# Layer 1 of a fused attention and MLP kernel: one set of four tiles by half products in blocks 3 to 6, fixed staging tiles, and another place for the check of the bounds

## The chip, the cores and the metric

The kernel runs on one core of a Trainium2 chip. Its time is the device time of one execution in microseconds; several runs are given by their median. The engines are called TensorE (PE in the profile, its weight loads PEld), VectorE (DVE), ScalarE (ACT), GpSimd (POOL) and SyncE (SP).

## The reference

Eight batches of 576 tokens. Attention of 8 heads of 64 columns each, causal, with 16 beacon keys and values in front that every token sees; then a low-rank mix over the tokens, and a two-layer MLP with a residual:

```python
scores = scale * q @ concat(beacon_k, k).T        # causal on k; beacons always seen
a = softmax(scores);  x = a @ concat(beacon_v, v) # x: (8, 576, 512) after joining the heads
u = x + ((x.T @ U) @ V).T                         # U (576, 32), V (32, 576)
out = u + relu(u @ w_ch1) @ w_ch2                 # w_ch1 (512, 2048), w_ch2 (2048, 512), float32 out
```

The kernel computes in 16-bit floats with sums in float32.

## The kernel before, in words

**Two interleaved streams.** The attention goes by pairs of heads (`p` = 4 x batch + pair), the MLP by nine blocks of 512 tokens out of the 4608. The MLP's work is cut into units, closures in a list `queue`; `fill(n)` takes n of them and issues their instructions. The order of issue is written out by hand: `long_slot` (L1383) gives for each pair of heads from batch 3 on where the scores (`go`), the masks, the weighting of the two heads (`weighted`), the mix and the `fill`s stand. One batch takes 30 units, and a block has 30. The pattern of one batch puts units 3 to 12 of a block beside pair 3, units 13 to 15 and the first two of layer 2 beside pair 0, the next nine beside pair 1, and the rest and units 0 to 2 of the next block beside pair 2. Every engine works through its own instructions in the order of issue.

**Layer 1.** `g_unit(k)` (L628): 16 units for 16 tiles of 128 of the 2048 hidden columns; each is four matmuls of 512 tokens into one PSUM bank (L635), then a rectifying eviction to the tile `gT` on ScalarE (L646) or, in units 2, 5, 11 and 13, on VectorE (L644). `u` lies transposed in a ring `uT` of 4 x 576 columns (L163); where a block crosses the ring's end, in block 4 at its middle, each matmul is two of 256 columns (`u_cols`, L165).

**Layer 2.** A product of 512 x 2048 by 2048 x 512, done as seven products of halves instead of eight (`products`, L827). `sums` (L617) builds on VectorE the sums of halves of `gT` that this takes (L624); `SUMS` (L1164) says after which unit, with 16 and up for layer 2. `c_unit(k, j)` (L833) is half j of product k, 14 units, called c0 to c13 here; `after(k)` (L795) adds the banks into the four quarters of the output (L780) with float32 tiles of the ring `kept` (three buffers), adds the residual on GpSimd (`residual`, L791) and stores. Quarter 22 is ready at c9, 21 at c11, 12 at c13.

**Blocks 7 and 8** (`QUADS`, L1163) do layer 1 otherwise (`g_quads`, L649): three sets q of four tiles (2q, 2q+1, 8+2q, 9+2q) are products of halves as well, seven of 256 columns instead of eight, in four steps (`step`, L696), and four tiles are left as plain ones. Such a set needs four sums of weights, made ahead on GpSimd (`quad_weights`, L580), and the block needs four sums of `u`, made on VectorE (L655) in its units 0, 2 and 3. A bank A collects products over all four steps, and ScalarE copies it out after each of the first three (L686) and rectifies it after the last (L715); banks F and D take the others, and VectorE adds a copy to a bank on its way to `gT` (L689) and rectifies (L694). In step 1 the half product on A reads the second sum of `u`. These blocks do layer 2 by `chain_units` (L842), where the second product grows in the banks of the first (`grown`, L847), evicted by halves (L864). Block 7 has 29 units, block 8 has 31.

**Banks.** `pst` (L108) hands out the eight PSUM banks in the order in which they were given back (`emptying`); a bank's next matmul waits until the last reader has finished.

**Staging.** Keys and queries of a batch are loaded by GpSimd's DMAs to two tiles of a pool `stage` with two buffers each (`qk_tiles`, L253): six rows of 512 columns for batches 0 to 3 (`emit_loads`), five of six for the later ones (`load_whole`, L1029). `quad_tiles` (L569) takes further tiles of the pool for the sums of weights and of `u` and for the copies.

**The mix and the end.** `mix` (L1208) puts the units of the low-rank mix into the queue and spreads four empty entries (None) behind. For the last batch, all that is left of block 6 at that time is units 10 to 15 and c0 to c13, and blocks 7 and 8 follow. `guard` (L997) is the check of the bounds: nine VectorE instructions over the reciprocals `rec` of all heads (a memset, three pairs of comparisons, a reduction, a comparison); `guard_sum` (L1009) sums the result on TensorE, and a branch to a safe path is taken on it at the end.

Of the kernel before, what the change touches and what calls it, by code (L numbers as in the profile page):

```python
# [9 lines left out]
F16 = mybir.dt.float16  # L10
# [8 lines left out]
P = 128  # L19
# [11 lines left out]
def kernel(  # L31
# [61 lines left out]
    stage = ctx.enter_context(tc.tile_pool(name="stage", bufs=2))  # L93
# [354 lines left out]
    def mix_units(xb, u0, turned=True):  # L448
# [47 lines left out]
        def end():  # L496
# [9 lines left out]
            settle(1, uT[:, :, ds(u0 % RING + QM, n)], ups)  # L506
            emptying(ups)
# [71 lines left out]

    def quad_weights(q):  # L580
# [5 lines left out]
        s1, s2, s3, s4 = lq["w"][q]  # L586
# [8 lines left out]
    def fast_units(t0, dst, last=False, quads=False):  # L595


        cell, banks, obs = {}, {}, {}
        cols = u_cols(t0, 512)
# [28 lines left out]
        def g_unit(k):  # L628
            if k == 0:
                begin()  # L630
            dc = order[k]
# [7 lines left out]
            if k % 2 and cell["turns"]:  # L639
                cell["turns"].pop(0)()  # L640
            for x in SUMS.get(k, ()):
                sums(*x)
            if k in (2, 5, 11, 13):
# [5 lines left out]
        def g_quads():  # L649

            at = t0 % RING
            b11, b12, b21, b22 = (uT[:, ds(c, 2), ds(at + x, HT)] for c in (0, 2) for x in (0, HT))
            t1, t2, t3, t4 = lq["t"]
            us = [
                lambda o=o, x=x, y=y: nc.vector.tensor_tensor(out=o, in0=x, in1=y, op=ALU.subtract)  # L655
                for o, x, y in ((t1, b12, b11), (t2, b22, t1), (t3, b22, b12), (t4, b21, t2))
            ]
            held = {}

            def plain(dc):  # L660
                g = pst([P, 512], F32, name="gps")
                for cc in range(NCC):
                    nc.tensor.matmul(  # L663
                        g, w1[:, cc, ts(dc, P)], uT[:, cc, ds(at, 512)], start=cc == 0, stop=cc == NCC - 1
                    )
                nc.scalar.activation(out=cell["g"][:, dc, :], in_=g, func=AF.Relu)
                emptying(g)
# [14 lines left out]
            def of_lw(q, k):  # L682
                return lambda c, i: lq["w"][q][k][:, c, ts(i, P)]

            def copied(q, k):
                nc.scalar.activation(out=lq["k"][q][k], in_=held[q, "A"], func=AF.Copy)  # L686

            def summed(q, bank, k, d, x):
                nc.vector.tensor_tensor(  # L689
                    out=cell["g"][:, ds(d, 2), ds(x, HT)], in0=held[q, bank], in1=lq["k"][q][k], op=ALU.add  # L690
# [30 lines left out]

            slots = [
# [6 lines left out]
            def unit(k, slot):  # L729
# [4 lines left out]
                if isinstance(slot, int):  # L734
                    plain(slot)
# [11 lines left out]
        sums_at = {k - NDC: x for k, x in SUMS.items()}  # L747

# [83 lines left out]

        def c_unit(k, j):  # L833
# [731 lines left out]
```

## Time and profile before

| | |
|---|---|
| Time, median of 3 runs | 335.93 us (335.27 to 336.42) |
| The profiled execution | 336.39 us |
| Its span in the profile | 334.5 us |
| TensorE busy | 326.3 us |
| VectorE busy | 251.7 us |
| ScalarE busy | 190.8 us |
| GpSimd busy | 148.5 us |
| Block 3 begins at, block 7 begins at | 146.0 us, 279.3 us |

The profile is of one execution. Its times count from the start of the span; a group or a timeline row names line, engine, operation and tiles (out<-in), and what ended the idle time ahead of it. "L635" is line 635 of the code above.

### The profile page before, as it was taken

The numbers are of one execution on the slowest core, as the hardware profiler recorded it, in microseconds if no ns is written. First come the engines' busy times: TensorE is split into PE (matmuls) and PEld (weight loads), VectorE is DVE, ScalarE is ACT, GpSimd is POOL, SyncE is SP. The second block draws the span as 40 slices with busy tenths as digits, with TensorE's granted clock in tenths as the row PEclk, the third lists the DMA queues.
The fourth block names the chain that finished last, engine by engine and source line by source line (L and its number), as shares of the span: only waits on it lengthen the run. The fifth ranks groups of instructions, "written<-read, shape, count | busy, mean of one in ns | idle before, by whom it ended". The sixth has DMA issues, their size and how long they took to land.

```text
span 334.5 us, 9085 instructions
## 1 busy us (share of the span) xinstructions
PE 326.3 (98%) x3614; PEld 223.9 (67%) x3614; DVE 251.7 (75%) x572; ACT 190.8 (57%) x413; POOL 148.5 (44%) x185
## 2 busy tenths in 40 slices
PE   8899999999999999999999999999999999999993
PEld 3565555555577656865588888754875588788793
DVE  6675888678897668765777677667777978797692
ACT  5967961788972677257734684469435403703700
POOL 8987824766236540677066904150398014010010
PEclk9999999999999999999999999999999999999999
DMA  8999999999999993999999996955213513206113
GB/s 164 144 176 161 158 201 196 199 184 151 81 150 150 135 181 74 130 200 171 151 124 174 144 132 110 117 130 120 51 42 94 91 47 110 49 32 127 31 36 101
DMA packets 150561, 41.99 MB, mean 126 GB/s; under 512 B 131312, under 2 KB 149936, under 8 KB 150512
## 3 DMA queue, kind: packets, MB, share of 16 engines
q0 software_dynamic: 87568, 18.18, 73.3%
q1 hardware_dynamic: 62144, 22.41, 36.5%
q10 hardware_dynamic: 800, 0.75, 0.7%
q8 instruction: 30, 0.49, 0.6%
q14 instruction: 19, 0.16, 0.2%
HBM read 37.45 MB, written 9.44 MB: 140 GB/s over the span
## 4 chain that ended last, share of the span: by engine, by line
PE 91%; ACT 5%; DVE 1%; issue 0%
PE gps L635 24%; PE po L427 8%; PE mpsD L760 6%; PE sps L409 6%; PE mpsF L760 4%; PE cps L965 4%; PE mpsA L854 4%; PE gps L939 4%; PE mpsE L760 3%; PE qpsA L674 3%; PE mpsC L760 3%; PE mpsA L760 3%; PE mpsB L760 3%; ACT expt L376 2%; PE mpsD L854 2%; PE gps L663 2%
## 5 line engine op out<-in xcount | busy, mean ns | idle before, releaser
L418 ACT ACTIVATE expt<-sps 128x496 f16<-128x496 f32 (+2 forms) x192 | 82.2, 547 | 41.6 <-PE sps L409 41.6
L635 PE MATMUL gps<-uT,w 128*128 128x512 f16 (+1 forms) x448 | 91.9, 349 | 0.2 <-ACT kT L1091 0.2
L780 POOL TENSOR_TENSOR ob<-ob,ut 128x512 f32<-128x512 f32 x26 | 31.3, 1207 | 131.2 <-DVE ob L780 121.5
L760 PEld LDWEIGHTS <-gT 128*128 128x128 f16 x704 | 66.4, 98 | 10.4 <-issue 2.6
L635 PEld LDWEIGHTS <-w 128*128 128x128 f16 x448 | 40.4, 98 | 32.0 <-issue 2.5
L646 ACT ACTIVATE gT<-gps 128x512 f16<-128x512 f32 x72 | 42.9, 619 | 25.2 <-PE gps L635 19.9
L624 DVE TENSOR_TENSOR gT<-gT 128x1024 f16<-128x1024 f16 (+3 forms) x90 | 47.5, 550 | 1.0
L240 POOL DMA_DIRECT2D vs<-in_v_dram x50 | 39.9, 812 | 14.1 <-DMA w<-in_moe_w_ch_dram 11.1
L427 PEld LDWEIGHTS <-expt 128*128 128x128 f16 x900 | 33.8, 98 | 9.8 <-issue 1.5
L427 PE MATMUL po<-vs,expt 128*128 128x65 f16 x900 | 36.4, 194 | 0.3
L348 DVE TENSOR_TENSOR expt<-expt,bigmask 128x768 f16<-128x768 f16 x54 | 34.4, 676 | 1.4 <-ACT expt L418 1.2
L436 DVE TENSOR_TENSOR xb<-po,rec 128x320 f16<-128x320 f32 x64 | 31.5, 492 | 2.2
L435 DVE RECIPROCAL rec<-po 128x5 f32<-128x5 f32 x64 | 12.1, 189 | 19.5 <-PE po L427 19.1
L644 DVE TENSOR_SCALAR gT<-gps 128x512 f16<-128x512 f32 x24 | 16.6, 690 | 13.1 <-PE gps L635 12.6
L686 ACT ACTIVATE lk<-qpsA 128x512 f32<-128x512 f32 x18 | 10.3, 597 | 25.6 <-PE qpsA L674 14.8
L409 PE MATMUL sps<-qT,kT 64*128 64x80 f16 (+4 forms) x288 | 22.6, 281 | 0.0
L376 ACT ACTIVATE expt<-sps 128x496 f16<-128x496 f32 (+2 forms) x48 | 20.4, 569 | 0.7 <-PE sps L370 0.7
L854 PEld LDWEIGHTS <-gT 128*128 128x128 f16 x208 | 19.0, 98 | 2.4
L1038 POOL DMA_DIRECT2D st<-in_q_dram x20 | 16.9, 866 | 6.9 <-DVE ob L780 6.5
L409 PEld LDWEIGHTS <-kT 64*128 64x128 f16 x288 | 10.3, 94 | 12.8 <-issue 8.2
L1038 POOL DMA_DIRECT2D st<-in_k_dram x20 | 16.9, 859 | 1.5 <-DMA st<-in_q_dram 1.5
L939 PE MATMUL gps<-uT,w 128*128 128x512 f16 x64 | 16.2, 380 | 0.1
(151 smaller groups left out, 479.3 us busy)
## 6 DMA issues: line engine op xcount, KB each, us to landing
out_dram<-ob SPq DMA_DIRECT2D x33, 256.0 KB, 3.6
vs<-in_v_dram POOLq DMA_DIRECT2D x18, 128.0 KB, 6.9
w<-in_moe_w_ch_dram POOLq DMA_DIRECT2D x4, 512.0 KB, 6.4
w<-in_moe_w_ch_dram POOLq DMA_DIRECT2D x2, 1024.0 KB, 12.8
st<-in_k_dram POOLq DMA_DIRECT2D x12, 128.0 KB, 6.3
st<-in_q_dram POOLq DMA_DIRECT2D x12, 128.0 KB, 7.0
st<-in_k_dram POOLq DMA_DIRECT2D x4, 288.0 KB, 11.8
st<-in_q_dram POOLq DMA_DIRECT2D x4, 288.0 KB, 12.9
```

What stands on the lines that cost most here:

```text
L240: nc.gpsimd.dma_start(out=dst[a : a + nq[j], j, :, :], in_=src[hs, ds(q0[j], nq[j]), :].rearrange("h p d -> p h d"))
L348: nc.vector.tensor_tensor(out=e, in0=e, in1=bigmask[:, :, :].rearrange("p (a b) x -> p a b x", b=2), op=ALU.min)
L409: nc.tensor.matmul(banks[i][:, ds(at0 + o, w)], kT(hp, c, ch), qT[hp, c, ds(qa, w)], start=True, stop=True, skip_group_check=len(unit) > 1,)
L418: nc.scalar.activation(out=at[p][3][i][:, ds(AT[g], gw[g])], in_=bank[:, ds(at0, gw[g])], func=AF.Exp, scale=scale)
L427: nc.tensor.matmul(po[:, j, :], ex[0 : nk[c], ds(blk[(c, j)], P)], vs[0 : nk[c], ds(c * H * E + h * E, E)], start=(c == 0), stop=(c == j),)
L436: nc.vector.tensor_tensor(out=xb[:, :, ds(h * D, D)], in0=po[:, :, 0:D], in1=r.broadcast_to([P, NT, D]), op=ALU.mult)
L624: nc.vector.tensor_tensor(out=o[:, ds(d0, n)], in0=x[:, ds(d0, n)], in1=y[:, ds(d0, n)], op=op)
L635: nc.tensor.matmul(g[:, ds(o, w)], w1[:, cc, ts(dc, P)], uT[:, cc, ds(at, w)], start=(cc == 0 and o == 0), stop=(cc == NCC - 1), skip_grou ...
L646: nc.scalar.activation(out=cell["g"][:, dc, :], in_=g, func=AF.Relu)
L760: nc.tensor.matmul(ps, a()[:, d, ds(P * i, P)], bm[:, d, ds(c0, w)], start=fresh and d == 0 and i == 0, stop=d == HF - 1, skip_group_check ...
L854: nc.tensor.matmul(ps, a()[:, d, ds(P * i, P)], bm[:, d, ds(c0, w)], start=fresh and d == 0, stop=d == HF - 1, skip_group_check=True,)
L1038: coming.append(lambda d=dst, s=src, a=m[j] - nq[j], n=m[j], j=j: nc.gpsimd.dma_start(out=d[a:n, j, :, :], in_=s[:, ds(q0[j], nq[j]), :].r ...
```

## The change

In blocks 3 to 6 the tiles 0, 1, 8 and 9 of layer 1 become one set of half products (`PARTS` is 1 there); the other twelve stay plain, three of them evicted on VectorE (units 2, 11 and 13) and nine on ScalarE. The block still has 16 units for layer 1, the four steps standing in units 1, 3, 6 and 8. The four sums of `u` for block t are issued on VectorE in c10 to c13 of block t - 1 (`AHEAD`). Four of the sums of `gT` come later (at units 11, 12, 13 and c2 instead of 8, 9, 10 and 12), the others where they were. The first two products of layer 2 go as in `chain_units`: the second grows in the first one's banks, and ScalarE evicts both by halves; VectorE's add for quarter 11 goes.

The pool `stage` is replaced by four fixed tiles. The sums of `u` lie in their last 512 columns, which the later batches' loads don't touch. The sums of weights of the first set lie in the pool `pairs` and are made in batch 3 (`P6 + 3`) instead of batch 7; its copies lie in the ring `kept`, also in blocks 7 and 8. The other two sets take the staging tiles at the old time.

`guard` is put into the queue 66 entries before its end instead of being issued when the last mix is queued, and `guard_sum` 34 entries before the end instead of 37.

```diff
-    def qk_tiles():
-        t = [stage.tile([P, TJ * DM], F16, name=f"st{i}", tag=f"st{i}") for i in range(2)]
+    staged = [const.tile([P, TJ * DM], F16, name=f"st{i}", tag=f"st{i}") for i in range(4)]
+    def qk_tiles(b=0):
+        t = staged[2 * (b % 2) : 2 * (b % 2) + 2]
...
-    lq = {}
-    def quad_tiles():
-        t = [stage.tile([P, TJ * DM], F16, name=f"lw{i}", tag=f"st{i}") for i in range(2)]
-        w = [[x[:, ds(512 * k, 512)] for k in range(4)] for x in t]
-        w.append([pairs.tile([P, 512], F16, name=f"lw{k}", tag=f"pr{k % 2}") for k in range(4)])
-        lq["w"] = [[x.rearrange("p (c f) -> p c f", c=2) for x in y] for y in w]
-        lq["t"] = [x[:, ds(4 * 512 + 512 * k, 512)].rearrange("p (c x) -> p c x", c=2) for x in t for k in range(2)]
-        f = [stage.tile([P, 3, 512], F32, name=f"lk{i}", tag=f"st{i}") for i in range(2)]
-        k = [x[:, i, :].rearrange("p (i x) -> p i x", i=2) for x in f for i in range(3)]
-        lq["k"] = [(k[2 * q], k[2 * q + 1], k[2 * q]) for q in range(3)]
+    lq, settled = {}, set()
+    def quad_tiles(q):
+        if q == 0:
+            w = [pairs.tile([P, 512], F16, name=f"lw{k}", tag=f"pr{k % 2}") for k in range(4)]
+        else:
+            w = [staged[q - 1][:, ds(512 * k, 512)] for k in range(4)]
+            f = staged[q + 1][:, 0 : 2048].bitcast(F32).rearrange("p (k i x) -> p k i x", k=2, i=2)
+            lq["k", q] = (f[:, 0], f[:, 1], f[:, 0])
+        lq["w", q] = [x.rearrange("p (c f) -> p c f", c=2) for x in w]
+    def u_half(t0, c0, x):
+        return uT[:, ds(c0, 2), ds((t0 + x) % RING, HT)]
+    def u_sums(t0, eng):
+        b11, b12, b21, b22 = (u_half(t0, c, x) for c in (0, 2) for x in (0, HT))
+        t1, t2, t3, t4 = (staged[i][:, 5 * DM : 6 * DM].rearrange("p (c x) -> p c x", c=2) for i in range(4))
+        lq["t"] = [t1, t2, t3, t4]
+        def one(o, x, y):
+            assert (t0 + 511) // S in settled
+            eng.tensor_tensor(out=o, in0=x, in1=y, op=ALU.subtract)
+        return [lambda a=a: one(*a) for a in ((t1, b12, b11), (t2, b22, t1), (t3, b22, b12), (t4, b21, t2))]
...
+        def layer_one(dc, on_vector, between=lambda: None):
...
+            between()
+            if on_vector:
                 nc.vector.tensor_scalar_max(out=cell["g"][:, dc, :], in0=g, scalar1=0.0)
             else:
                 nc.scalar.activation(out=cell["g"][:, dc, :], in_=g, func=AF.Relu)
...
+            def plain(k, dc):
+                layer_one(dc, not quads and k in (2, 11, 13))
...
+            def space(q, k):
+                if k < 2:
+                    cell["k", q, k] = lq["k", q][k] if q else kept("k")
+                else:
+                    cell["k", q, k] = cell["k", q, 0]
+                return cell["k", q, k]
...
-                nc.scalar.activation(out=lq["k"][q][k], in_=held[q, "A"], func=AF.Copy)
+                nc.scalar.activation(out=space(q, k), in_=held[q, "A"], func=AF.Copy)
...
+            if not quads:
+                slots = [2, (0, 0), 10, (0, 1), 3, 11, (0, 2), 4, (0, 3), 12, 5, 13, 6, 14, 7, 15]
+                late = {11: ((0, 0, 4),), 12: ((1, 0, 4),), 13: ((2, 0, 4),), 14: ((0, 4, 3),), 15: ((1, 4, 3),)}
+                def unit(k, slot):
+                    if k == 0:
+                        begin()
+                    plain(k, slot) if isinstance(slot, int) else step(*slot)
+                    if k % 2 and cell["turns"]:
+                        cell["turns"].pop(0)()
+                    for x in late.get(k, ()):
+                        sums(*x)
+                return [lambda k=k, slot=slot: unit(k, slot) for k, slot in enumerate(slots)]
...
+        if parts:
+            sums_at = {0: ((2, 4, 3),), 1: ((0, 7, 1), (1, 7, 1)), 2: ((2, 7, 1), (3, 0, 4)), 3: ((3, 4, 4),)}
...
+        def grown(k, name, i, c0, w):
...
+        def first(i, c0, w):
+            ps = grown(0, "A", i, c0, w)
+            if i == 0:
+                kept("s1")
+            nc.scalar.activation(out=cell["s1"][:, i, :], in_=ps, func=AF.Copy)
+        def second_on(i, c0, w):
+            ps = grown(1, "A", i, c0, w)
+            if i == 0:
+                out_tile("11")
+            nc.scalar.activation(out=obs["11"][:, i, :], in_=ps, func=AF.Copy)
+            freed(("A", i, c0))
+            if i:
+                residual("11", 0, 0)
         def c_unit(k, j):
-            bank = products[k][0]
-            p = pieces(bank)[j]
-            product(*products[k], *p)
+            p = pieces(products[k][0])[j]
+            if parts and k < 2:
+                (first, second_on)[k](*p)
+            else:
+                product(*products[k], *p)
             for x in sums_at.get(2 * k + j, ()):
                 sums(*x)
-            if j == 1:
+            for u in ahead(2 * k + j) if ahead else ():
+                u()
+            if j == 1 and not (parts and k < 2):
                 after(k)
...
-        units = [lambda k=k: g_unit(k) for k in range(NDC)]
+        units = g_quads() if parts else [lambda k=k: g_unit(k) for k in range(NDC)]
...
-    QUADS = (7, 8)
+    PARTS = {3: 1, 4: 1, 5: 1, 6: 1, 7: 3, 8: 3}
+    AHEAD = 10
...
+    def sums_ahead(t):
+        if PARTS.get(t, 0) != 1:
+            return None
+        us = []
+        def at(n):
+            if n == AHEAD:
+                us.extend(u_sums(512 * t, nc.vector))
+            return us[n - AHEAD : n - AHEAD + 1] if n >= AHEAD else []
+        return at
...
-                units = fast_units(512 * t, dst, t == NBLK - 1, t in QUADS)
+                units = fast_units(512 * t, dst, t == NBLK - 1, PARTS.get(t, 0), sums_ahead(t + 1))
...
+            if p == P6 + 3:
+                quad_tiles(0)
+                coming.extend(quad_weights(0))
             if p == NP - 3:
-                quad_tiles()
-                coming.extend([u for q in range(3) for u in quad_weights(q)])
+                for n in (1, 2):
+                    quad_tiles(n)
+                    coming.extend(quad_weights(n))
...
         mix(B - 1)
-        guard()
-        queue.insert(len(queue) - 37, guard_sum)
+        queue.insert(len(queue) - 66, guard)
+        queue.insert(len(queue) - 34, guard_sum)
```

More of the change, by code (lines that the diff above doesn't have):

```diff
@@ L649, in g_quads @@
         def g_quads():
-            at = t0 % RING
-            b11, b12, b21, b22 = (uT[:, ds(c, 2), ds(at + x, HT)] for c in (0, 2) for x in (0, HT))
+            b11, b12, b21, b22 = (u_half(t0, c, x) for c in (0, 2) for x in (0, HT))
+            us = u_sums(t0, nc.vector)
             t1, t2, t3, t4 = lq["t"]
[L654 to L657, printed above, removed]
             held = {}
[L660 to L667, printed above, removed]
+            def plain(k, dc):
+                layer_one(dc, not quads and k in (2, 11, 13))
             def half(q, bank, a, b, fresh):
@@ L845, in chain_units @@
             small = [(0, 0, HC), (1, 0, P), (1, P, P)] if last else halves
-            def grown(k, name, i, c0, w):
-                _, a, bm, _ = products[k]
-                fresh = (name, i, c0) not in banks
-                if fresh:
-                    banks[name, i, c0] = pst([P, w], F32, name="mps" + name)
-                ps = banks[name, i, c0]
-                for d in range(HF):
-                    nc.tensor.matmul(
-                        ps, a()[:, d, ds(P * i, P)], bm[:, d, ds(c0, w)],
-                        start=fresh and d == 0, stop=d == HF - 1, skip_group_check=True,
-                    )
-                return ps
-            def first(i, c0, w):
-                ps = grown(0, "A", i, c0, w)
-                if i == 0:
-                    kept("s1")
-                nc.scalar.activation(out=cell["s1"][:, i, :], in_=ps, func=AF.Copy)
             def second(i, c0, w):
```

42 lines of the change are left out of this document (27 added, 15 removed).

## The prediction

> **What bounds the kernel now.** I read the page first: the busy line of part 1 and the shares of the chain of part 4.
>
> ```profile
> PE 326.3 (98%) x3614; PEld 223.9 (67%) x3614; DVE 251.7 (75%) x572; ACT 190.8 (57%) x413; POOL 148.5 (44%) x185
> PE 91%; ACT 5%; DVE 1%; issue 0%
> ```
>
> TensorE is busy for 98% of the span, and the chain that ended last is TensorE for 91%. A busy share is an average, so I next asked for the windows of blocks 3 to 7, one row for each block.
>
> ```profile
> core 0: us, PE busy (x) PEld busy (x) DVE busy (x) ACT busy (x) POOL busy (x), PEclk, DMA share, GB/s
> 146.00:180.50 34.50, 34.50 (x373) 22.77 (x372) 24.70 (x52) 20.76 (x45) 18.36 (x22) 1.00 1.76 162
> 180.50:215.30 34.80, 34.80 (x438) 29.04 (x437) 24.84 (x52) 20.77 (x45) 16.50 (x20) 1.00 1.50 135
> 215.30:249.90 34.60, 34.60 (x374) 22.78 (x372) 24.99 (x52) 20.76 (x45) 14.82 (x13) 1.00 0.47 82
> 249.90:279.30 29.40, 29.40 (x272) 19.60 (x271) 23.43 (x47) 8.74 (x15) 11.36 (x10) 1.00 0.32 75
> 279.30:305.00 25.70, 25.70 (x220) 21.15 (x219) 22.11 (x45) 10.09 (x19) 2.68 (x3) 1.00 0.28 84
> ```
>
> In all five TensorE fills its window at clock 1.00. So a matmul taken out of blocks 3 to 6 shortens the run by its spacing, and a wait put in front of a matmul lengthens it by its length: there is no slack behind TensorE to lose it in. VectorE has about 10 us free in each of blocks 3 to 5, but only 6 us in block 6 and 3.6 us in block 7.
>
> **What the change takes away.** The price of a matmul is its spacing in an unbroken run; I read it from the chain in order of time (start, length, count).
>
> ```profile
> 184.64 4.47 PE gps L635 x40
> 259.93 6.05 PE gps L635 x28
> 284.63 1.31 PE qpsA L674 x12
> ```
>
> A 512-wide matmul costs 6.05/28 = 0.216 us, a 256-wide half product 1.31/12 = 0.109 us. Four plain tiles are 16 matmuls, 16 x 0.216 = 3.46 us; by half products they are 7 x 4 = 28 matmuls, 28 x 0.109 = 3.06 us. That is 0.40 us less in each of blocks 3, 5 and 6. In block 4 the token ring ends inside the block, so its plain tiles already are 256 wide (the row with 40 in 4.47 us); there 32 become 28, 4 x 0.109 = 0.44 us. **Taken from TensorE: 1.64 us.** Layer 2 keeps its matmuls: its second product now grows in the first one's banks, with as many matmuls as before.
>
> **What it adds elsewhere.** The prices stand in the groups by form (count, total, mean ns).
>
> ```profile
> L644 DVE TENSOR_SCALAR gT<-gps 128x512 f16<-128x512 f32 x24 | 16.6, 690 | 13.1 <-PE gps L635 12.6
> L689 DVE TENSOR_TENSOR gT<-qpsD,lk 128x512 f16<-128x512 f32 x12 | 7.9, 685 | 4.1 <-ACT lk L686 2.2 <-PE qpsD L674 1.9
> L694 DVE TENSOR_SCALAR gT<-gT 128x1024 f16<-128x1024 f16 x6 | 2.6, 427 | 0.2
> L694 DVE TENSOR_SCALAR gT<-gT 128x512 f16<-128x512 f16 x6 | 1.8, 294 | 0.2
> L655 DVE TENSOR_TENSOR lw<-uT 128x512 f16<-128x512 f16 x4 | 1.7, 418 | 0.0
> L780 DVE TENSOR_TENSOR ob<-mpsF,kept 128x512 f32<-128x512 f32 x8 | 5.5, 691 | 4.4 <-PE mpsF L760 4.4
> L646 ACT ACTIVATE gT<-gps 128x512 f16<-128x512 f32 x72 | 42.9, 619 | 25.2 <-PE gps L635 19.9 <-issue 4.3 <-ACT ob L980 0.7
> L686 ACT ACTIVATE lk<-qpsA 128x512 f32<-128x512 f32 x18 | 10.3, 597 | 25.6 <-PE qpsA L674 14.8 <-DVE ob L780 10.7
> L864 ACT ACTIVATE kept<-mpsA 128x256 f32<-128x256 f32 x4 | 1.5, 384 | 1.5 <-PE mpsA L854 1.5
> ```
>
> VectorE per block: four sums of u, 4 x 0.418 = 1.67 us; three sums onto banks, 3 x 0.685 = 2.05; two rectifications, 0.29 + 0.43 = 0.72; less one eviction (0.69) and the add of output quarter 11 (0.69): 3.06 us more, some 28 us in 34. ScalarE: three copies and a rectification of a bank (4 x 0.60, all as L686) for three evictions (3 x 0.62), and four half copies (4 x 0.384) for one whole (0.60, as L686): about 1.5 us more, some 22 in 34. Neither becomes the bound by its total, so what counts is where an instruction is late.
>
> I placed the new order on the old times, engine by engine. Three places could be tight. The first is the start of block 4 (rows: VectorE's and GpSimd's timeline, the chain, and the groups for a head's two VectorE instructions).
>
> ```profile
> 179.55 1.98 DVE L348 TENSOR_TENSOR expt<-expt,bigmask 128x768 f16<-128x768 f16 x2
> 179.71 1.40 POOL L780 TENSOR_TENSOR ob<-ob,ut 128x512 f32<-128x512 f32 x1 [1.40 <-DVE ob L780]
> ...
> 180.58 0.87 PE gps L635 x8
> ...
> L436 DVE TENSOR_TENSOR xb<-po,rec 128x320 f16<-128x320 f32 x64 | 31.5, 492 | 2.2
> L435 DVE RECIPROCAL rec<-po 128x5 f32<-128x5 f32 x64 | 12.1, 189 | 19.5 <-PE po L427 19.1
> ```
>
> With two banks held, unit 4 takes the bank that the second weighted head left. VectorE gets there after the masks (179.55 + 1.98 = 181.5), two sums of u (0.8), the add of c13 (0.6), a head (0.7), the quad's first sum and rectification (0.9) and the second head (0.7): 185.2. TensorE starts unit 4 after units 0 to 3 (4 x 0.87), two heads (2 x 0.46) and the scores (0.5): 180.58 + 4.9 = 185.5. So it just fits, at no cost. The second place: held banks A and D leave six of eight, and the scores ask for six at once only after unit 8 has given both back. The third: in unit 8 the second half product grows in bank D, which VectorE must have read with the copy that ScalarE made in unit 6.
>
> ```profile
> 219.18 2.01 ACT L418 ACTIVATE expt<-sps 128x496 f16<-128x496 f32 x4 [1.04 <-PE sps L409]
> 221.05 1.12 ACT L646 ACTIVATE gT<-gps 128x512 f16<-128x512 f32 x2
> 223.78 0.46 PE po L427 x15
> ```
>
> From the end of unit 6 to that half product TensorE has unit 7 (0.865), the weighting of one head (0.46) and another half product (0.44): 1.76 us of cover. The way round is the copy (0.60), the sum (0.69) and, as I estimate, 0.2 to ScalarE and 0.1 at each later hand-over: 1.7 us, and up to 0.2 more if ScalarE, which still works off the four exponentials of the first row, has the eviction of unit 5 ahead of the copy. So between 0 and 0.16 us in each of blocks 3 to 5, nothing in block 6 where ScalarE has idle time: 0 to 0.5 us. I take **0.2 us**. The first set's four weight sums on GpSimd move from blocks 5 and 6 to block 2, behind the loads that are queued there; unit 3 of block 3 needs them about a block later (34 us), and no load of that time is awaited by TensorE: nothing. The fixed tiles cost nothing as long as the sums' columns and the loads' columns don't wait for each other (a rival below).
>
> **The check that moves.** The check of the bounds is nine VectorE instructions. Here are its first, its last and the one behind it, from VectorE's timeline of block 6.
>
> ```profile
> 261.30 0.33 DVE L999 MEMSET good<- 128x320 f16 x1
> ...
> 263.87 0.16 DVE L1007 TENSOR_SCALAR bad<-allg 128x1 f16<-128x1 f32 x1
> 263.94 0.68 DVE L624 TENSOR_TENSOR gT<-gT 128x1024 f16<-128x1024 f16 x1
> ```
>
> It holds VectorE for 263.94 - 261.30 = 2.64 us, and there TensorE didn't notice. The change puts it 66 entries before the queue's end. Blocks 7 and 8 have 29 and 31 units; the mix of the last batch leaves unit c11, an empty entry, c12, an empty one, c13 and two empty ones ahead of them. So six of these seven follow, and the check comes right behind c11, two units before block 7. That place I read closely.
>
> ```profile
> 277.63 0.69 DVE L780 TENSOR_TENSOR ob<-mpsE,kept 128x512 f32<-128x512 f32 x1
> 279.38 0.69 DVE L780 TENSOR_TENSOR ob<-mpsD,kept 128x512 f32<-128x512 f32 x1 [1.05 <-PE mpsD L760]
> 279.99 0.41 DVE L655 TENSOR_TENSOR lw<-uT 128x512 f16<-128x512 f16 x1
> 280.44 1.26 DVE L655 TENSOR_TENSOR lw<-uT,lw 128x512 f16<-128x512 f16 x1
> ...
> 277.20 2.37 POOL L780 TENSOR_TENSOR ob<-ob,ut 128x512 f32<-128x512 f32 x2 [5.59 <-DVE ob L780]
> 280.15 1.27 POOL L780 TENSOR_TENSOR ob<-ob,ut 128x512 f32<-128x512 f32 x1 [0.59 <-DVE ob L780]
> ...
> 281.46 0.43 PE qpsF L674 x4
> 281.89 0.55 PE qpsA L674 x4
> ```
>
> The second sum of u (280.44) ends at 281.70, and the half product that reads it starts at 281.89; 0.55 instead of 0.44 says that TensorE already waited 0.11 us for it. So whatever makes VectorE later here goes into the time one for one. VectorE starts the add of c11 at 277.63 and could go on at 277.63 + 0.61 = 278.24; the add of c13 starts at 279.38, after its idle time. So 1.14 us of the check are hidden and 2.64 - 1.14 = **1.50 us** are not. The sum at 280.44 took 1.26 instead of 0.42 us because GpSimd's add of 280.15 runs until 281.42; it follows the add of c13, so it comes along unchanged. ScalarE's first copy of block 7 now lies in the ring of three "kept" tiles and reuses the one that the add of c13 reads, so it starts after that add; its reader on VectorE stands behind the second sum of u anyway, so this has no price of its own.
>
> The check can be held in the same way: GpSimd's second add of the pair runs until 277.20 + 2.37 = 279.57, and the check's third instruction, the first that reads two tensors, would stand at about 278.9. I take 279.57 - 278.9 = **0.65 us** for that; nothing is the other end, as before has no check beside a GpSimd add, and 1.0 if the check's second instruction is held too. I take the hold, because the masks of 179.55 are nearest to it: two reads of two tensors, with GpSimd's add of 179.71 in between, and 1.98 us for both. [...]
>
> **The sum:** -1.64 + 0.2 + 1.50 + 0.65 = +0.7 us. Against the profiled execution (336.39 us, of it 334.5 span) that is 337.1; that execution lies 0.46 us above the median of 335.93, so for the median I say **336.6 us**. By its own bounds (waits 0 to 0.5, hold 0 to 1.0) the forecast runs from -0.1 to +1.4: 335.8 to 337.3.
>
> **The rivals.** 1. *The check is hidden.* If TensorE reaches block 7 with VectorE ahead, or the check's place isn't the one I counted, only the saving and the waits of unit 8 stand: -1.64 + 0.2 = -1.4, 334.5 us. For it speaks that all of block 6's layer 2 has idle VectorE time; against it that the add of c11, which paces the check, waits for TensorE's own c11.
> 2. *VectorE and ScalarE are late in every block* (the slower side). Place: unit 8 of blocks 3 to 5, and unit 10, which takes the bank of the head weighted just before. It decides from the point at which ScalarE's copy of unit 6 is more than 0.1 us later than I have it; from there each delay goes to TensorE. If the eviction of unit 4, too, stands ahead of the copy (another 0.5 us), that is 0.5 in each of three blocks, +1.3 beside my 0.2: 337.9 us. For it: VectorE at 28 of 34 us, and sums of u that GpSimd can hold (1.26 instead of 0.42). Against: in my placing VectorE sits idle for about 2 us before unit 6's sum.
> 3. *The change doesn't do what it says:* the sums of u, now in the loads' own tiles, wait for the loads of a later batch (part 6 of the page: 288 KB, median time from issue to landing).
>
> ```profile
> st<-in_k_dram POOLq DMA_DIRECT2D x4, 288.0 KB, 11.8
> ```
>
> One landing awaited in full is 11.8 us on VectorE, of which at most the 10 us free in a block hide something: some 2 to 12 us, 339 to 348 us. Against it: the ring of u is a fixed tile used in parts already, and TensorE reads and VectorE writes it side by side.
>
> **Chances.** The forecast 0.47, rival 1 0.15, rival 2 0.28, rival 3 0.10. About 0.3%, 1.0 us, is what a measurement can tell from no change. Faster by more than that is rival 1 without its edge: 0.13. Slower takes rival 3, rival 2 but for its edge (0.25) and the upper end of the forecast (0.07): 0.42. The rest, 0.45, lies within. The range goes from 334.9, which leaves out most of rival 1, to 338.0, which leaves out rival 3 and the edge of rival 2: about 0.2 outside.
>
> **What would show it.** Right: the chain's pieces of blocks 3 to 6 with 0.4 us less each; in block 7 the first half product that reads a sum of u starts about 2 us later after its predecessor; the check's instructions between the adds of c11 and c13, over 2.64 us in all, one of them long. Wrong: a gap of TensorE at unit 8 or 10 of each block (rival 2), VectorE waiting for a DMA ahead of a sum of u (rival 3), or block 7 without a gap (rival 1).

## The result, and the profile after

Before: 335.66 us (22 runs, 335.21 to 336.42). After: 337.94 us (22 runs, 335.87 to 338.79). The ratio is 1.0051, with an interval of 1.0036 to 1.0067: slower by half a per cent. The forecast was 336.6 us. The 22 runs of after fall into two groups with nothing between: eight from 335.87 to 336.45 at a mean clock of 0.997 to 1.000, and fourteen from 337.74 to 338.79 at 0.991 to 0.995. None of the 22 of before lies above 336.42. The profiled execution (337.74 us, span 336.1) is of the larger group.

The page of after, the busy line and the chain by engine:

```profile
PE 326.5 (97%) x3646; PEld 227.8 (68%) x3646; DVE 265.0 (79%) x600; ACT 195.8 (58%) x429; POOL 149.1 (44%) x185
PE 86%; DVE 7%; ACT 5%; issue 1%; DVEq 0%
```

VectorE now holds 7% of the chain, where it held 1%. The windows of blocks 3 to 7, cut at each block's first matmul (length first, then busy time by engine, then the granted clock), say where:

```profile
145.78:179.96 34.18, 34.18 (x387) 24.00 (x385) 27.74 (x59) 21.93 (x49) 18.55 (x22) 1.00 1.69 152
179.96:214.27 34.31, 34.31 (x434) 28.62 (x432) 26.94 (x60) 21.95 (x49) 16.42 (x20) 1.00 1.57 140
214.27:248.45 34.18, 34.18 (x385) 23.93 (x384) 28.72 (x57) 21.94 (x49) 14.70 (x13) 1.00 0.42 86
248.45:277.88 29.43, 29.28 (x284) 20.86 (x283) 23.57 (x46) 10.14 (x19) 6.97 (x6) 1.00 0.33 75
277.88:306.89 29.01, 26.82 (x216) 21.49 (x214) 23.75 (x51) 10.00 (x18) 2.70 (x3) 0.94 0.25 68
```

By the same cuts (in the chain of before at 146.00, 180.58, 215.32, 249.90, 279.27 and 304.43 us) the five blocks took 34.58, 34.74, 34.58, 29.37 and 25.16 us. So blocks 3 to 5 save 0.40, 0.43 and 0.40, block 6 loses 0.06 where it should save 0.40, and block 7 loses 3.85 us. Only in the last two rows is TensorE busy for less than its window, and only in the last is the clock below 1. In block 7, TensorE's timeline:

```profile
279.90 0.60 PE L690 MATMUL qpsF<-uT,w 128*128 128x256 f16 x4
282.69 1.04 PE L690 MATMUL qpsA<-st,lw 128*128 128x256 f16 x4 [2.19 <-DVE st L593]
...
286.04 0.60 PE L690 MATMUL qpsA<-st 128*128 128x256 f16 x4
286.48 0.60 PE L690 MATMUL qpsD<-st,st 128*128 128x256 f16 x4
```

The half product that reads the second sum of `u` waits 2.19 us, as forecast. From there on four groups of half products, from 282.69 to 286.04, take 0.84 us each instead of 0.44 (286.04 to 286.48): about 1.6 us more that the forecast didn't have. The windows of one microsecond show why (the granted clock is the third number from the end):

```profile
282.00:283.00 1.00, 0.31 (x2) 0.25 (x3) 1.00 (x2) 0.00 (x0) 0.35 (x1) 0.79 0.00 0
283.00:284.00 1.00, 1.00 (x7) 0.69 (x6) 0.96 (x3) 0.19 (x1) 0.00 (x0) 0.50 0.72 240
...
286.00:287.00 1.00, 1.00 (x11) 0.88 (x10) 0.09 (x1) 0.39 (x2) 0.00 (x0) 1.00 0.56 65
```

After TensorE's rest of 2.19 us the granted clock is 0.50. A mean of 0.79 is 0.58 us at 1.00 and 0.42 us at 0.50, so it falls at 282.58 and is back at 286.00: 3.42 us. In 336 us that makes a mean clock of 0.995, and 0.992 with the fall that the profile also shows behind the last matmul; so the mean clocks of the fourteen slower executions fit one such fall in each, though only one of them has a profile. Why TensorE rested, from VectorE's and then GpSimd's timeline:

```profile
276.24 0.69 DVE L820 TENSOR_TENSOR ob<-mpsE,kept 128x512 f32<-128x512 f32 x1
276.95 0.33 DVE L1053 MEMSET good<- 128x320 f16 x1
277.31 0.97 DVE L1056 TENSOR_SCALAR good<-rec 112x64 f16<-112x64 f32 x1
278.32 0.34 DVE L1057 SCALAR_TENSOR_TENSOR good<-rec,good 112x64 f16<-112x64 f32 x1
...
280.24 0.16 DVE L1061 TENSOR_SCALAR bad<-allg 128x1 f16<-128x1 f32 x1
280.32 0.69 DVE L820 TENSOR_TENSOR ob<-mpsD,kept 128x512 f32<-128x512 f32 x1
280.93 0.41 DVE L593 TENSOR_TENSOR st<-uT 128x512 f16<-128x512 f16 x1
281.37 1.26 DVE L593 TENSOR_TENSOR st<-uT,st 128x512 f16<-128x512 f16 x1
```

```profile
275.80 2.36 POOL L820 TENSOR_TENSOR ob<-ob,ut 128x512 f32<-128x512 f32 x2 [6.07 <-DVE ob L820]
281.09 1.26 POOL L820 TENSOR_TENSOR ob<-ob,ut 128x512 f32<-128x512 f32 x1 [2.92 <-DVE ob L820]
```

The check stands between the adds of c11 and c13, as counted, and one of its instructions takes 0.97 us (0.26 in before, at 261.66) and lasts until GpSimd's pair has ended (275.80 + 2.36 = 278.16): it is the second, not the third. Block 6's loss, from VectorE, GpSimd and TensorE:

```profile
244.89 1.03 DVE L593 TENSOR_TENSOR st<-uT 128x512 f16<-128x512 f16 x1
245.95 1.26 DVE L593 TENSOR_TENSOR st<-uT,st 128x512 f16<-128x512 f16 x1
...
247.74 2.34 DVE L349 TENSOR_TENSOR expt<-expt,bigmask 128x768 f16<-128x768 f16 x2
250.00 1.38 DVE L593 TENSOR_TENSOR st<-uT 128x512 f16<-128x512 f16 x1
251.30 0.41 DVE L593 TENSOR_TENSOR st<-uT,st 128x512 f16<-128x512 f16 x1
251.63 0.68 DVE L820 TENSOR_TENSOR ob<-mpsD,kept 128x512 f32<-128x512 f32 x1
```

```profile
244.49 1.15 POOL L605 TENSOR_TENSOR st<-st,w 128x512 f16<-128x512 f16 x1
245.59 1.34 POOL L605 TENSOR_TENSOR st<-w 128x512 f16<-128x512 f16 x1
246.89 1.34 POOL L820 TENSOR_TENSOR ob<-ob,ut 128x512 f32<-128x512 f32 x1
248.19 1.47 POOL L605 TENSOR_TENSOR st<-w,st 128x512 f16<-128x512 f16 x1
249.62 1.47 POOL L820 TENSOR_TENSOR ob<-ob,ut 128x512 f32<-128x512 f32 x1
```

```profile
251.90 0.31 PE L410 MATMUL sps<-qT,kT 64*128 64x336 f16 x1
252.36 0.37 PE L410 MATMUL sps<-qT,kT 64*128 64x336 f16 x5 [0.15 <-DVE ob L820]
252.67 0.50 PE L690 MATMUL qpsA<-st,lw 128*128 128x256 f16 x3
```

VectorE works without a pause from 244 to 253 us; the four sums of `u` take 1.03, 1.26, 1.38 and 0.41 us instead of 0.42 each, with GpSimd's weight sums of sets 2 and 3 and its residual adds beside them. So the add of c13 gives its bank back late, and the scores of block 6 wait for it: these six matmuls take from 251.90 to 252.67, 0.77 us. Where block 6 has no sums of `u` (an experiment below) the same six take 0.32 us (251.84 to 252.16). The difference, 0.45 us, is block 6's loss.

### The profile page after: what moved, and what is told of

Read it like the earlier page. It is cut to its first block, busy times and chain, and to the rows that moved or that the text cites. A ratio compares the mean times of both kernels' runs of the same rounds, so it can differ in the third digit from the quotient of the medians.

```text
span 336.1 us, 9192 instructions
## 1 busy us (share of the span) xinstructions
PE 326.5 (97%) x3646; PEld 227.8 (68%) x3646; DVE 265.0 (79%) x600; ACT 195.8 (58%) x429; POOL 149.1 (44%) x185
## 4 chain that ended last, share of the span: by engine, by line
PE 86%; DVE 7%; ACT 5%; issue 1%; DVEq 0%
PE gps L664 21%; PE mpsA L880 8%; PE po L428 8%; PE sps L410 6%; PE qpsA L690 5%; PE mpsD L800 5%; PE cps L1019 4%; PE gps L993 4%; PE mpsB L800 3%; PE qpsD L690 3%; PE mpsE L800 3%; PE mpsC L800 3%; ACT expt L377 2%; PE mpsF L800 2%; PE mpsD L880 2%; ACT w L377 2%
## 5 line engine op out<-in xcount | busy, mean ns | idle before, releaser
L664 PE MATMUL gps<-uT,w 128*128 128x512 f16 (+1 forms) x400 | 84.9, 354 | 0.2 <-ACT kT L1145 0.2
L664 PEld LDWEIGHTS <-w 128*128 128x128 f16 x400 | 36.6, 98 | 28.9 <-issue 1.8
L672 ACT ACTIVATE gT<-gps 128x512 f16<-128x512 f32 x68 | 40.6, 618 | 19.6 <-PE gps L664 14.1
L709 ACT ACTIVATE kept<-qpsA 128x512 f32<-128x512 f32 x18 | 10.8, 602 | 25.6 <-PE qpsA L690 14.9
L670 DVE TENSOR_SCALAR gT<-gps 128x512 f16<-128x512 f32 x20 | 13.8, 689 | 11.7 <-PE gps L664 11.4
L880 PE MATMUL mpsA<-w,gT 128*128 128x256 f16 x160 | 19.0, 273 | 0.0
L712 DVE TENSOR_TENSOR gT<-qpsD,kept 128x512 f16<-128x512 f32 x12 | 8.3, 692 | 11.6 <-ACT kept L709 9.0
```

What stands on the lines that cost most here:

```text
L664: nc.tensor.matmul(g[:, ds(o, w)], w1[:, cc, ts(dc, P)], uT[:, cc, ds(at, w)], start=(cc == 0 and o == 0), stop=(cc == NCC - 1), skip_grou ...
L880: nc.tensor.matmul(ps, a()[:, d, ds(P * i, P)], bm[:, d, ds(c0, w)], start=fresh and d == 0, stop=d == HF - 1, skip_group_check=True,)
```

## The experiments

These runs were made in four lots, each with its own executions of the kernel before (medians 335.66 to 335.80 us); each ratio is to those of its own lot. The names in brackets are those by which the expectations speak of the runs.

**The check alone.** (Run guard_alone.) The kernel before, with only the check's place moved.

```diff
-        guard()
-        queue.insert(len(queue) - 37, guard_sum)
+        queue.insert(len(queue) - 66, guard)
+        queue.insert(len(queue) - 34, guard_sum)
```

> The kernel before with only the check of the bounds moved to its new place (the sum of the check with it). Theory (the check's place costs the time): a gap of TensorE of about 2.1 us ahead of the first half product of block 7 that reads a sum of u, so 337.8 us where the granted clock stays at 1.00, and some 1.8 us more, 339.6, in the executions in which the clock falls behind the gap as in the changed kernel's profile. Rival (the half products in blocks 3 to 6 cost it, by a VectorE that is late): 335.7, no gap.

Measured: 338.39 us, ratio 1.0081 (1.0061 to 1.0100). Four runs lie at 337.98 to 338.40 and two at 339.59 and 340.00, the last with its profile. TensorE's rest there is 2.28 us, and the clock falls too, but later, when TensorE is at work again:

```profile
284.00:285.00 1.00, 0.83 (x8) 0.78 (x9) 0.96 (x4) 0.20 (x1) 0.00 (x0) 1.00 0.33 114
285.00:286.00 1.00, 1.00 (x7) 0.72 (x6) 0.96 (x3) 0.40 (x1) 0.00 (x0) 0.50 1.03 279
...
288.00:289.00 1.00, 1.00 (x10) 0.79 (x7) 0.00 (x0) 0.47 (x1) 0.00 (x0) 0.79 0.58 131
```

By the same working it is down from 285.0 to 288.42, 3.42 us again. So the check's place alone, without a half product in blocks 3 to 6, brings the rest and the fall: the rest is worth 2.4 us (the middle of the four runs, 338.2, less 335.8) and the fall 1.6 on top (339.8 less 338.2).

**The check where it was.** (Run guard_back.) The changed kernel, the check issued as before.

```diff
-        queue.insert(len(queue) - 66, guard)
+        guard()
```

> The changed kernel with the check issued where it was before, when the last mix is queued. Theory: the 2.2 us gap of block 7 and the fall of the clock go, 1.2 us of the four blocks' saving stay: 334.4 us (334.2 to 334.9), unless VectorE, fuller now in block 6, makes layer 2 wait for a sum there (up to 1 us, 335.4). Rival (half products cost): still 336 or more.

Measured: 334.13 us (333.67 to 334.61), ratio 0.9949 (0.9933 to 0.9965). The rest of the change is a gain. In the profile TensorE doesn't rest in block 7:

```profile
280.10 0.60 PE L690 MATMUL qpsF<-uT,w 128*128 128x256 f16 x4
280.56 0.61 PE L690 MATMUL qpsA<-st,lw 128*128 128x256 f16 x4
```

**The check behind c3** (guard_c3), where VectorE waits for TensorE between its adds.

```diff
-        queue.insert(len(queue) - 66, guard)
+        queue.insert(10, guard)
```

> The changed kernel with the check behind c3 of block 6, where VectorE sits idle for 2.1 us ahead of the add of c4. Theory: 334.4 us, and no wait of layer 2 in block 6; the add of c4 some 0.6 us later, unnoticed. Rival (half products cost): 336 or more.

Measured: 334.31 us, ratio 0.9957 (0.9940 to 0.9973), not told apart from the place before. So putting the check into the queue costs nothing by itself; its place ahead of the adds that block 7 waits for does.

**TensorE kept busy in the rest** (warm_gap), with ten 512-wide matmuls into a spare bank.

```diff
+        def busy():
+            ps = pst([P, 512], F32, name="idle")
+            for _ in range(10):
+                nc.tensor.matmul(ps, w1[:, 0, 0:P], w1[:, 0, 0:512], start=True, stop=True)
+            emptying(ps)
+        queue.insert(len(queue) - 57, busy)
```

> The changed kernel with ten more 512-wide matmuls into a spare bank (10 x 0.216 = 2.16 us, their result unused) in the gap of block 7, behind the third unit. Theory (the clock falls because TensorE rests): every execution at 1.00 and the time that of the changed kernel's faster executions, 336.1 us, not less and not more than 0.3 more. Rival (the clock falls for another cause, the kernel's denser work): still two kinds of executions, 336.2 and 338.1.

Measured: 336.36 us, ratio 1.0026 (1.0011 to 1.0041). Ten of twelve runs lie between 336.25 and 336.46 at clocks of 0.997 up, at the upper end of after's eight faster ones; the other two, 337.48 (0.997) and 338.83 (0.994), stay unexplained. In the profile the added matmuls fill the rest:

```profile
280.50 2.32 PE L1534 MATMUL idle<-w 128*128 128x512 f16 x10
282.86 0.61 PE L690 MATMUL qpsA<-st,lw 128*128 128x256 f16 x4
```

The half products that read the second sum of `u` start no earlier than in after, but with TensorE at work the clock stays up (1.00 from 279.3 to 305 us): the rest lowers the clock, not the half products.

**A shorter and a longer rest.** (Runs gap_small and gap_large.) Two of the check's three pieces left out, and all three done twice.

```diff
-        for rr, jj in ((nq[0], slice(0, 1)), (P, slice(1, 4)), (nq[4], slice(4, 5))):
+        for rr, jj in ((nq[0], slice(0, 1)),):
```

> The changed kernel with two of the three pieces of the check left out (four of its nine VectorE instructions, about 1.04 us; the values of those pieces are not looked at). The gap of TensorE in block 7 shrinks from 2.19 to about 1.1 us. Theory (the clock falls because of the length of TensorE's rest): the granted clock stays 1.00 and every run is the same: 336.1 (the runs of the changed kernel without the fall) less 1.05, 335.0 us. Rival (any rest over about a microsecond at this place lets it fall in two runs of three): 335.0 in some runs, 336.9 in most.

```diff
-        for rr, jj in ((nq[0], slice(0, 1)), (P, slice(1, 4)), (nq[4], slice(4, 5))):
+        for rr, jj in ((nq[0], slice(0, 1)), (P, slice(1, 4)), (nq[4], slice(4, 5))) * 2:
```

> The changed kernel with the three pieces of the check done twice (six more VectorE instructions, about 1.6 us). The gap of TensorE becomes about 3.8 us. Theory (clock falls by the length of the rest, two in three at 2.2 us): now it falls in all runs; 336.1 + 1.6 + 1.9 = 339.6 us. Rival (the fall does not depend on the length: again one third of the runs without it): 337.7 in a third of the runs and 339.6 in the rest.

Measured, shorter: 335.53 us, ratio 0.9993 (0.9963 to 1.0024); the rest is 1.17 us, and ten of twelve runs lie at 334.93 to 335.88 with clocks of 0.997 up, half a microsecond above what was expected of them. The two at 337.73 and 338.87 say little: in this lot four of 29 runs of the kernel before, which has no such rest, and three of twelve of tiles_only lie above 337 as well, six of these seven at clocks of 0.989 to 0.995. None of them has a profile, so what happened there stays open. Longer: 339.96 us, ratio 1.0117 (1.0075 to 1.0160); no run has a clock above 0.994, and three lie at 339.2 to 339.3 (0.991 to 0.994), three at 340.6 to 341.7 (0.987 to 0.989). Its profile is of the second group:

```profile
282.00:283.00 1.00, 0.00 (x0) 0.00 (x0) 0.97 (x3) 0.00 (x0) 0.28 (x1) 0.93 0.00 0
...
289.00:290.00 1.00, 1.00 (x8) 0.78 (x7) 0.00 (x0) 0.40 (x1) 0.00 (x0) 0.65 0.43 97
```

With a rest of 3.68 us the clock is down from 282.86 to 289.70: 6.84 us, twice 3.42. So, as far as these counts go, the length of the rest decides how often the clock falls (1.17 us: not told from the kernel without a rest; 2.2: in fourteen runs of 22 in after, in two of six in the first experiment; 3.68: in all six), and the fall comes in pieces of one length. The expectation's 339.6 for all runs missed the double piece.

**The fixed tiles alone** (tiles_only): no half products in blocks 3 to 6, the check where it was.

```diff
-    PARTS = {3: 1, 4: 1, 5: 1, 6: 1, 7: 3, 8: 3}
+    PARTS = {7: 3, 8: 3}
...
-        queue.insert(len(queue) - 66, guard)
+        guard()
```

> The changed kernel without the half products in blocks 3 to 6 (no sums of u there, no product grown in place) and with the check of the bounds issued where it was before: what is left of the change are the fixed staging tiles and the eviction order of blocks 7 and 8. Theory (fixed tiles cost nothing, the half products save 1.6 us): as the kernel before, 335.7 us. Rival (the fixed tiles, or the earlier weight sums, themselves save or cost several tenths, and the half products less or more): 335.2 or below, or 336.2 or above.

Measured: 335.31 us, ratio 0.9993 (0.9957 to 1.0029). No cost is seen, and a gain of up to 0.4 us by the medians isn't told from none. The half products are then worth about 335.31 - 334.13 = 1.2 us (two lots, whose kernels before differ by 0.1 us), not 1.64: it fits three blocks' savings (0.40 + 0.43 + 0.40 = 1.23) and nothing from block 6.

**Block 6 without half products** (no_block6), the check where it was.

```diff
-    PARTS = {3: 1, 4: 1, 5: 1, 6: 1, 7: 3, 8: 3}
+    PARTS = {3: 1, 4: 1, 5: 1, 7: 3, 8: 3}
...
-        queue.insert(len(queue) - 66, guard)
+        guard()
```

> The changed kernel with the check where it was before, and with half products in blocks 3 to 5 alone; block 6 runs as in the kernel before. Theory (block 6's half products bring nothing, because their sums of u are held): 334.1 us, the same as guard_back. Rival (they do save 0.4 us, and block 6 loses it elsewhere): 334.5 us.

Measured: 333.97 us, ratio 0.9955 (0.9938 to 0.9973). Block 6's set brings nothing that is seen, as the theory had it; this is the fastest median of all, though not told apart from 334.13.

**The weight sums earlier** (best2), all eight of them in block 5 (the check where it was, here and in the next ones).

```diff
-            if p == NP - 3:
+            if p == NP - 5:
```

> The changed kernel with the check of the bounds issued where it was before (as in guard_back, 334.13 us), and GpSimd's eight weight sums of sets 2 and 3 two heads earlier, so that they run in block 5 instead of at the end of block 5 and the start of block 6. Theory (the missing 0.4 us of block 6 is lost because these sums hold VectorE's masks and sums of u of block 6): the held instructions of about 245 to 251 us become short, the scores of block 6 don't wait, block 6 is 0.4 us shorter: 333.7 us. Rival (the loss only moves: in block 5 the masks and head instructions of VectorE are held instead, and TensorE waits there): 334.1 us, block 5 longer by what block 6 gains. Second rival (block 6 is short of VectorE time with or without the holds): 334.1 us, block 5 unchanged and the wait of the scores still there.

Measured: 336.51 us, ratio 1.0022 (0.9999 to 1.0045): 2.4 us slower than with the sums at their old time. Block 6, though, from 251.17 to 280.15 us, took 28.98 us: the missing 0.4 us is there (the block's first and last piece of the chain):

```profile
251.17 0.86 PE gps L664 x4
278.40 1.75 PE mpsD L800 x16
```

The four sums of `u` now take 0.41, 1.26, 0.41 and 0.41 us, the long one beside a residual add, and the scores don't wait. With no_block6, where block 6 took 29.37 us (248.41 to 277.78) as in before, this shows both halves of the cause: neither the weight sums without sums of `u` nor sums of `u` without the weight sums cost block 6 time, only the two side by side. Block 5 (214.19 to 251.17) took 36.98 us instead of after's 34.18. In VectorE's timeline of block 5, and GpSimd's:

```profile
229.63 2.94 DVE L349 TENSOR_TENSOR expt<-expt,bigmask 128x768 f16<-128x768 f16 x2
232.49 1.65 DVE L642 TENSOR_TENSOR gT<-gT 128x1024 f16<-128x1024 f16 x1
```

```profile
229.11 1.61 POOL L605 TENSOR_TENSOR st<-st,w 128x512 f16<-128x512 f16 x1
230.69 1.46 POOL L605 TENSOR_TENSOR st<-w 128x512 f16<-128x512 f16 x1
232.12 1.47 POOL L605 TENSOR_TENSOR st<-w,st 128x512 f16<-128x512 f16 x1
```

Two masks take 2.94 instead of 1.02 us and a sum of `gT` 1.65 instead of 0.68: the rival, worse than it said.

**The weight sums later** (weights_u4 and weights_mix), in two ways that were meant to differ. In both profiles GpSimd makes the eight sums in the same place, right behind the last residual add of block 5's output, so they count as two measurements of one order.

```diff
-            if p == NP - 3:
-                for n in (1, 2):
-                    quad_tiles(n)
-                    coming.extend(quad_weights(n))
...
+            if t == 6:
+                for n in (1, 2):
+                    quad_tiles(n)
+                ws = quad_weights(1) + quad_weights(2)
+                for i, w in enumerate(ws):
+                    units[4 + i] = lambda a=units[4 + i], w=w: (a(), w())
```

> The changed kernel with the check of the bounds where it was before (as in guard_back, 334.13 us) and GpSimd's eight weight sums of sets 2 and 3 issued later, one in each of units 4 to 11 of block 6, behind the sums of u of block 6 and most of its masks. In best2, with the same sums earlier, block 6 did become 0.39 us shorter than before, but block 5 lost over 2 us to VectorE's held masks. Theory (these sums cost where VectorE is busy with instructions that they hold; in layer 1 of block 6 VectorE has room): the sums of u at about 245 to 251 us take 0.41 us each, block 6 is 0.4 us shorter and block 5 as in guard_back: 333.7 us. Rival (they hold VectorE wherever they are put: the masks of 255 us, the check or layer 1's sums run late into layer 2): 334.1 us or above.

```diff
-            if p == NP - 3:
-                for n in (1, 2):
-                    quad_tiles(n)
-                    coming.extend(quad_weights(n))
...
         guard()
+        for n in (1, 2):
+            quad_tiles(n)
+            coming.extend(quad_weights(n))
```

> As weights_u4, but the eight weight sums come later still, behind the check of the bounds, from about 262 us on, where layer 1's two-input sums of VectorE stand back to back (263 to 269 us). Theory: block 6's first half is 0.4 us shorter as in weights_u4, but the sums of 263 to 269 us are held by up to 1 us each, so the products of layer 2 wait: 334.5 us or above. Rival (VectorE's room in layer 2 of block 6 takes it all): 333.7 us, as weights_u4.

Measured: 334.82 us, ratio 0.9975 (0.9966 to 0.9983), and 334.99, ratio 0.9981 (0.9971 to 0.9991). GpSimd made the sums at 252 to 262 us in the second's profile, and block 6 took 30.07 us (248.89 to 278.96). TensorE's timeline there:

```profile
258.29 0.60 PE L690 MATMUL qpsD<-uT,lw 128*128 128x256 f16 x4 [0.67 <-DVE gT L712]
```

Of the sums of `u` three take 0.41 us and one 1.26, as in best2, and the masks (2.90 us), a rectification (1.23) and a comparison of the check (1.23) are held instead, beside GpSimd (1.02, 0.29 and 0.26 us alone). VectorE's room in layer 1 of block 6 was not room: both runs are 0.7 to 0.9 us slower than guard_back, and 333.7, the theory of the one and the rival of the other, fell. The 334.5 or above of weights_mix came out, but not for its reason, since the sums ran some ten microseconds earlier than it had them.

**The weight sums split** (weights_split), four in block 5 and four at the old time.

```diff
+            if p == NP - 5:
+                quad_tiles(1)
+                coming.extend(quad_weights(1))
             if p == NP - 3:
-                for n in (1, 2):
-                    quad_tiles(n)
-                    coming.extend(quad_weights(n))
+                quad_tiles(2)
+                coming.extend(quad_weights(2))
```

> The changed kernel with the check where it was before (as guard_back, 334.13 us) and GpSimd's weight sums split: the four of set 2 issued in block 5 as in best2 (there the masks of 229.6 us were held only by the sums that ran after 229 us), the four of set 3 where they were. Theory (a sum of GpSimd costs only if a mask or a sum of u of VectorE stands beside it, so the masks of 229.6 us and the sums of u of 245 to 250 us are both free): block 5 as in guard_back, block 6 at most 29.0 us instead of 29.45 us, 333.7 us. Rival (some of the holds come back in one place or the other): 334.1 us or above.

Measured: 334.24 us, ratio 0.9958 (0.9934 to 0.9983). Block 6 (249.32 to 278.31) took 28.99 us, the full saving again, and the masks of 229.6 us were free. But what TensorE waited for in blocks 5 to 7, by the view of waits, was

```profile
PE gps L664 <- DVE xb L437: 0.5, 1, 0.5
PE sps L410 <- DMA qT<-st: 0.2, 1, 0.2
```

A rectification held at 224.6 us (1.19 instead of 0.43) made a head late, and 0.5 us went back in block 5. Whether some place for the eight sums costs nothing stays open; of the four tried (the old one among them), none gained in the time.

## Why the prediction was right, and where it wasn't

**Right.** The saving per block (0.40 and 0.43 forecast as 0.40 and 0.44) in blocks 3 to 5; no price for the banks, for the fixed tiles (within the interval) or, in after, for waits of the sums of `u` for loads; the check's place, its 1.50 us and a hold by GpSimd. The hold measured 0.97 - 0.26 = 0.71 us for 0.65, though on the second instruction, for which the forecast's upper bound had 1.0. The rest of 2.19 us against 1.50 + 0.65 = 2.15 is the forecast's own term.

**Luck in the number.** 337.94 lies above the forecast's own bounds (335.8 to 337.3). It is inside the range only because that was drawn up to 338.0 for rival 2, and it is all but rival 2's 337.9 us. But rival 2 didn't happen: blocks 3 to 5 are each shorter by what was forecast, with no gap of TensorE at unit 8 or 10. Two things that the forecast didn't have, below, brought the time there.

**The waits at unit 8** (0.2) were nothing: TensorE's busy time fills the windows of blocks 3 to 5, and in block 3 VectorE had read bank D by 153.69 + 0.69 = 154.38, ahead of the half product at 154.56. Of the hand-overs estimated at 0.2 and 0.1 us, before's timeline shows 0.20 to ScalarE (a group of four from 279.11, at 0.44, and its copy at 279.75), 0.03 on to VectorE (a copy from 285.10, at 0.60, and its sum at 285.73), and 0.15 from a sum of `u` to TensorE (281.70 to 281.85).

**Wrong, the saving of block 6.** The step that failed is what follows "Neither becomes the bound by its total": the four sums of `u` priced at 0.418 us each, and a list of three tight places without the scores of block 6. The total holds, but the sums of `u` of block 6 come where GpSimd's weight sums stand, at 240 to 250 us. I priced a hold for the check and named one for the sums of `u` in rival 2, but gave it no price in block 6. It cost 0.46 us (0.40 + 0.06); shown by block 6 at 28.98 and 28.99 us when weight sums stood elsewhere.

**Wrong, "into the time one for one".** A rest of TensorE isn't worth its length alone: in the profile, and by the clocks in fourteen of 22 runs, 3.42 us at half clock came with it, worth 1.6 us in the profile and 1.9 between the two groups. None of my rivals had that, and it makes most of the distance from 336.6 to 337.94: the eight runs without a fall lie at 336.1. Whether the median shows the fall was chance too, as 14 runs of 22 had it.

**The sum as it came out,** from the two profiled executions: -0.22 ahead of block 3, -1.23 in blocks 3 to 5, +0.06 in block 6, +3.85 in block 7 (2.19 of rest, about 1.6 of slow clock), and -0.86 behind block 7, where the end behind the last matmul was 5.16 us long in the execution of before and 4.31 in after's. Together +1.6, the spans' 336.1 - 334.5. That execution of before lies 0.7 us above its median, so its long end is no gain of the change.

By these runs, the version to keep is the changed kernel with the check where it was, with or without block 6's set: 334.13 or 333.97 us, ratio 0.9949 (0.9933 to 0.9965) or 0.9955 (0.9938 to 0.9973).

## What to carry to other kernels

Work that is moved to "somewhere in the queue" should land where its engine waits for the bound engine, not ahead of an instruction for which the bound engine waits: 2.6 us of VectorE cost nothing at one place and 2 to 4 us at another. Where TensorE is the bound, look at the granted clock behind each rest: here 2.19 us of rest came with 3.42 us at 0.50 in the profile, and the times fell into two groups 1.9 us apart; at 1.17 us none was told from chance. A sum on GpSimd had a price on VectorE here (sums of `u` of 1.03 to 1.38 us beside one instead of 0.42), so look at what stands beside it before counting VectorE's idle time as room.

## What the runs showed of the hardware

**The clock.** With a rest of 2.19 us the granted clock was 0.50 for 3.42 us; the fall began at 282.58 in after, 0.1 us ahead of the next matmul, and in the first experiment, with a rest of 2.28 us, at 285.0, 0.8 us behind it. So it isn't the end of the rest that starts it. It lasted 3.42 us in both, and 6.84, twice that, with the rest of 3.68 us. Behind the last matmul the clock falls once more, here in after and in before:

```profile
333.00:334.00 1.00, 0.00 (x0) 0.00 (x0) 0.00 (x0) 0.00 (x0) 0.00 (x0) 0.89 0.29 82
```

```profile
334.00:335.00 1.00, 0.00 (x0) 0.00 (x0) 0.00 (x0) 0.00 (x0) 0.00 (x0) 0.64 0.00 0
```

In after the last matmuls end at 331.79 (330.01 + 1.78 in the chain) and the clock falls at 333.78, after 1.99 us of rest. In before these stand at 329.34 (327.56 + 1.78) and 334.28, 4.94 us apart. So the fall doesn't come at one fixed time behind the last matmul either. After's two falls begin 51.20 us apart, which is 15 times 3.413, close to the length of one fall; that falls start only at such steps is my estimate from these two numbers, and one pair in one profile doesn't show it. Nor do these runs show what rest is enough, or why eight of after's 22 executions, by their clocks, escaped the fall.

**The hold.** A comparison on VectorE with one float32 tensor and a scalar was held beside GpSimd's add (in after 0.97 us at 277.31, in before 0.26 at 261.66 with no GpSimd add beside it), and a rectification of `gT` as well (in weights_mix 1.23 us at 252.36 beside a weight sum, in weights_split 0.29 at 252.80), not only instructions with two tensors (the sums of `u`, 1.03 to 1.38 us instead of 0.42).
